# Input rows loaded in longer runs and the contraction index split in pairs, in a gated mix of two attention branches

## The chip, the cores and the metric

The kernel runs on one core of a Trainium2 chip. The core has five engines with a program each: TensorE (PE, with its weight loads listed as PEld), VectorE (DVE), ScalarE (ACT), GpSimd (POOL) and SyncE (SP), which here issues every transfer. The metric is the device time of one execution, in microseconds; lower is better. The time before is the median of three runs, 845.19 us (843.88 to 845.63).

## The reference

The input x has 2048 rows of 512 values in bf16. Two branches read it, and a gate mixes them row by row:

```python
x = A_x
g = _sigmoid((x * gate_w).sum(-1, keepdims=True))
a = _A_ref(x, A_mem0, A_Wq, A_Wk, A_Wv, A_Wo, A_seg_len)
b = _B_ref(x, B_wq, B_wk, B_wv, B_wo, B_beta)
return g * a + (1 - g) * b
```

Branch A goes through 64 segments of 32 rows, one after another. Each puts 8 memory rows ahead of its rows, projects the 40 rows to queries, keys and values of 32 heads of 128, does masked attention, and projects the result back to 512 columns:

```python
for s in range(n_seg):
    h = jnp.concatenate([mem, xs], axis=1)
    q = jnp.einsum('btd,dhe->bhte', h, Wq)      # k and v likewise
    ...
    o = jnp.einsum('bhte,hed->btd', o, Wo)
    mem = o[:, :M, :].copy()
    outs.append(o[:, M:, :])
```

The first 8 rows of a segment's result are the memory of the next. The segments are therefore a chain.

Branch B projects x with three weights of 512 x 512 to 32 heads of 16, does causal attention inside each of 4 blocks of 512 rows, and adds what a running memory of key and value products from the blocks before gives; then it multiplies by wo.

## The kernel before

**Start.** `plan_warm` (L500) lets TensorE multiply zeros, `WARM` = 9 times. `plan_loads` (L515) issues the loads on SP in this order: the first 512 rows of x, the B weights wk, wq and wv, 512 more rows of x, three small inputs (beta, the gate weights, the memory rows), the rest of x. Rows of x lie in `x_sb`, which shares its memory with `Wo_sb`, and the profile calls it by that name; wvB is likewise `woB_sb`. Row tile i holds rows 128 i to 128 i + 127, one to a partition, so a load of two tiles reads runs of one row, 1 KB. The contraction index d of a weight is 128 c + p for partition p and c of 4, so a B weight is read in runs of 1 KB too. The A weights (Wk, Wq, Wv, 4 MB each in four loads of 1 MB with runs of 8 KB) are issued one at a time between the pieces of the B stage.

`x_chunk` (L561) turns 512 rows: for each half of a chunk, 8 transposes on TensorE (L573) write one bank, and two copies bring the bank to `xT`, with d on the partitions. Both copies of half 0 run on ACT (L390) and both of half 1 on DVE (L392). `evac` (L388) is the helper that records all such copies, so they share these two lines.

**B stage.** `b_projections` (L641) makes a list of pieces for the first three blocks. `pk` (L671) projects keys and queries, copies them to a stage tile `stgk` and stores them to DRAM through `store` (L653, the transfer itself is L654). `pv` (L689) projects 128 rows to values, copies them to `V17` and stores these, four stores a block, each in runs of 1,088 bytes. `kn` and `mz` make the running memory `MZ16`, which is stored as well. The main loop of `build` (L404 to L427) calls the pieces in order, and puts the chunks of x, the parts of the gate (`gate_parts`, L598: turn the gate weights, turn the memory rows, four sets of dot products) and the weight loads between them.

**A stage.** `plan_a` (L1251) plays lists of units written out by hand, one list for a group of four segments (`A_LIST0` to `A_LIST15`); every engine's program has the order of these lists. A unit is for instance a projection (L1281), the scores (L1542), P times V (L1607, L1619), the output projection (`out_part`, L1365), or `wl`, which issues one of eight loads of Wo. `LateB` (L767) projects B's last block with weights loaded 128 columns at a time (`load`, L779), and `BAttn` (L845) does B's attention, in the gaps. Scores of queries and keys use every second element of `KT_sb` and `QT_sb`, in which two heads are interleaved.

The output projection leaves four partial sums on four sets of 32 partitions. `fold` (L1376) adds and turns them: its stationary operand is 32 columns of the f32 tile `WF`, its moving operand a stack of identities, 8 matmuls for half the columns (16 in the trace). The copies `hm` put the first 8 rows into the next segment's `hT`, and `atx` and `aTl` put the rest into `aT_st`. That tile goes through DRAM (`aTd`) to `aTg`. `f_atr` in `tail_units` (L1477, the matmuls at L1482) turns it back into rows, 16 matmuls for a group of four segments, and the last step mixes in B's rows and the gate and stores the output.

**Memory.** The tiles of the start (`in_p`) and those of the A stage (`in_a`) lie over each other. `over` (L368) makes the first writer of an A tile wait for the last users of the start's tiles below it. In order of address the start's tiles are wkB, wqB, phK, etmp, bmask, mskT, mem0_sb, gwr_sb, beta_sb, gB_sb, omgB_sb, MZ16, stgk, V17.

SP works through its list in order: an issue that waits holds up all behind it.

Of the kernel before, what the change touches and what calls it, by code (L numbers as in the profile page):

```python
# [10 lines left out]
DEV = dict(nseg_limit=None)  # L11
WARM = 9

# [244 lines left out]
def build(nc, es, A_x, A_mem0, A_Wq, A_Wk, A_Wv, A_Wo, B_wq, B_wk, B_wv, B_wo, B_beta, gate_w, out, dbg=None):  # L258
    v = NS()
# [30 lines left out]
    def alloc(stack, *specs):  # L290
        at, spans = 0, {}
        for name, shape, dt, n in specs:
# [23 lines left out]
    in_p = alloc(esP, ("wkB", [128, C, DM], BF16, 0), ("wqB", [128, C, DM], BF16, 0), ("phK", [128, 4, DM], BF16, 0), ("etmp", [128, 512], BF16, 5),  # L316
          ("bmask", [128, 136], BF16, 0), ("mskT", [128, 2, 8, 2, 2], BF16, 0), ("mem0_sb", [128, DM], BF16, 0), ("gwr_sb", [128, 128], BF16, 0), ("beta_sb", [128, HB], BF16, 0),
          ("gB_sb", [128, HB], F32, 0), ("omgB_sb", [128, HB], F32, 0), ("MZ16", [128, 544], BF16, 0),
# [49 lines left out]
    def over(home):  # L368

        parts = {"mem0_sb": "mem0", "gwr_sb": "gwr", "beta_sb": "beta", "gB_sb": "gB", "omgB_sb": "omgB"}  # L370
        ops = []
        for p in v.under[home]:
            p = parts.get(p, p)
            for n, r in list(R.items()):
                if n == p or p in ("V17", "phK") and n.startswith(p) or p.startswith("stgk") and n[:-1] == p:
                    ops += ([r.w] if r.w else []) + r.readers
        return list({id(o): o for o in ops}.values())
# [27 lines left out]
    for n in range(len(pieces)):  # L405
        if n in (8, 20, 32):
            x_chunk(v, (n + 4) // 12)
        if n == 9:
            sigmoid(v, v.beta_sb[:, :], v.gB_sb, v.omgB_sb, "gB", [Rs("beta")])
            for src, dst, res in ((v.gB_sb, v.gBp, "gB"), (v.omgB_sb, v.omgBp, "omgB")):  # L410
                for j in range(4):
                    q = slice(32 * j, 32 * j + 32)
                    P.op("gp", lambda g, src=src, dst=dst, q=q, j=j: g.tensor_copy(dst[q, :].rearrange("p (f e) -> p f e", e=2), src[q, :].rearrange("p (f j e) -> p f j e", j=4, e=2)[:, :, j, :]),
                         reads=[Rs(res)], writes=[Rs(res + "p")], name="%sp%d" % (res, j))
            v.late_const()
        if n >= 36 and n % 2 == 0 and gates:
            gates.pop(0)()
        pieces[n]()
        if n == len(pieces) - 3:
            v.late_mask()  # L420
        if n in (36, 37, 38, 40, 42):
            bat.load(0, n // 2 % 2 if n != 37 else 0, "kv"[n // 40] if n != 37 else "q")
        if weights and n % 3 == 2:
            weights.pop(0)()
# [90 lines left out]
def plan_loads(v, A_x, A_mem0, A_Wq, A_Wk, A_Wv, B_wq, B_wk, B_wv, B_wo, B_beta, gate_w):  # L515
    P, Rs, C, M = v.P, v.Rs, v.C, v.M
    xsrc = A_x[0].rearrange("(i p) d -> p i d", p=128)

    def ld(grp, dst, src, res, name):
        P.dma(P.group(grp), lambda s: s.dma_start(dst, src), writes=[Rs(res)], name=name)  # L520

    def x(k):
        for h in range(2):
            o = 4 * k + 2 * h
            ld("x%d%d" % (k, h), v.x_sb[:, o:o + 2, :], xsrc[:, o:o + 2, :], "x_sb%d%d" % (k, h), "dma_x%d%d" % (k, h))
    x(0)
    for nm, dst, src in (("wk", v.wkB, B_wk), ("wq", v.wqB, B_wq), ("wv", v.wvB, B_wv)):
        ld("b" + nm, dst[:, :, :], src.rearrange("(c p) n -> p c n", p=128), nm + "B", "dma_" + nm)
    x(1)
    g = P.group("small")  # L530
    for fn, res in ((lambda s: s.dma_start(v.beta_sb[:, :], B_beta.rearrange("(o n) -> o n", o=1).to_broadcast([128, v.HB])), "beta"),
                    (lambda s: s.dma_start(v.gwr_sb[0:C, :], gate_w.rearrange("(c p) -> c p", p=128)), "gwr"),
                    (lambda s: s.dma_start(v.mem0_sb[0:M, :], A_mem0[0]), "mem0")):
        P.dma(g, fn, writes=[Rs(res)], name="dma_" + res)
# [3 lines left out]
    def weight(grp, dst, src, res, c):  # L538
        P.dma(grp, lambda s: s.dma_start(dst[:, c, :], src[c * 128:(c + 1) * 128].rearrange("p h e -> p (h e)")),
              writes=[Rs(res)], name="dma_%s%d" % (res, c))  # L540
# [18 lines left out]


def x_chunk(v, k):  # L561

    P, Rs, BK, C = v.P, v.Rs, v.BK, v.C
    for h in range(2):
# [3 lines left out]
        def f(pe, bk=bk, tiles=tiles):  # L568
            ins = None
            for n, i in enumerate(tiles):  # L570
                for c in range(C):
                    o = (n * C + c) * 128
                    ins = pe.transpose(v.pb16[bk][:, o:o + 128], v.x_sb[:, i, c * 128:(c + 1) * 128], v.ident[:, :])  # L573
            return ins
        P.op("pe", f, reads=[Rs("x_sb%d%d" % (k, h)), Rs("ident")], writes=[v.rbank[bk]], name="xtr%d_%d" % (k, h))
        t0 = 128 * tiles[0]
        dst = v.xT[:, :, t0:t0 + 256].rearrange("p c (n t) -> p n c t", t=128)
        src = v.pb16[bk][:, 0:1024].rearrange("p (n c t) -> p n c t", n=2, c=C)
        for n in range(2):
            v.evac("dve" if h else "act", dst[:, n, :, :], src[:, n, :, :], [bk], [Rs("xT%d_%d%d" % (k, h, n))], "xev%d_%d%d" % (k, h, n))  # L580
        BK.give(bk)
# [16 lines left out]
def gate_parts(v):  # L598

    P, Rs, BK, C, NTT = v.P, v.Rs, v.BK, v.C, v.NTT  # L600
    st = {}

    def weights():
        bk = BK.take()
        P.op("pe", lambda pe, bk=bk: pe.transpose(v.pb16[bk][:, 0:C], v.gwr_sb[0:C, :], v.ident[0:C, 0:C]),
             reads=[Rs("gwr"), Rs("ident")], writes=[v.rbank[bk]], name="gwtr")
        v.evac("dve", v.gw_sb[:, :], v.pb16[bk][:, 0:C], [bk], [Rs("gw")], "gwev")
        BK.give(bk)

# [17 lines left out]
    def memory():  # L627
        bk = BK.take()

        def f_m0tr(pe):  # L630
            ins = None
            for c in range(C):
                ins = pe.transpose(v.pb16[bk][:, c * v.M:(c + 1) * v.M], v.mem0_sb[0:v.M, c * 128:(c + 1) * 128], v.ident[0:v.M, 0:v.M])
            return ins
        P.op("pe", f_m0tr, reads=[Rs("mem0"), Rs("ident")], writes=[v.rbank[bk]], name="mem0tr")
        v.evac("dve", v.hT[0][:, :, 0:v.M], v.pb16[bk][:, 0:C * v.M].rearrange("p (c t) -> p c t", t=v.M), [bk], [Rs("hTm0_0"), Rs("hTm0_1")], "memT0")
        BK.give(bk)
    return [weights, memory] + [lambda k=k: dots(k) for k in range(NTT // 4)]


def b_projections(v):  # L641
# [47 lines left out]
    def pv(sb, tt):  # L689
# [3 lines left out]
        def fp(pe):  # L693
            ins = None
            for c in range(C):
# [4 lines left out]
        v.evac("act", v.V17[:, sb % 2, tt, :, 0:16].rearrange("p (e m) d -> p m e d", e=2), v.pb[bk].rearrange("p (m e d) -> p m e d", e=2, d=16), [bk], [rv], "evv%d_%d" % (sb, tt))  # L700
        store("stv%d" % sb, v.vd[sb, :, tt, :], v.V17[:, sb % 2, tt, :, :].rearrange("p h w -> p (h w)"), [rv, Rs("V17o")], [Rs("vd%d_%d" % (sb, tt))],
              "stv%d_%d" % (sb, tt))
        BK.give(bk)
# [63 lines left out]
class LateB:  # L767
# [11 lines left out]
    def load(self):  # L779
# [6 lines left out]
        m, f = self.work[4 + i]  # L786
        src = (v.B_wk if m == "K" else v.B_wq).rearrange("(c p) n -> p c n", p=128)[:, :, 128 * f:128 * (f + 1)]
        dst = v.woB_sb[:, i % 4, :].rearrange("p (c w) -> p c w", w=128)
        P.dma(P.group("lw%d" % i, "lw%d" % (i % 4)), lambda s: s.dma_start(dst, src), writes=[Rs("woc%d" % (i % 4))] + ([Rs("wvB")] if i < 4 else []), name="ldc%d" % i)

# [460 lines left out]
def plan_a(v, nseg):  # L1251
# [124 lines left out]
    def fold(bk, hf, part, res, name):  # L1376

        def f(pe):
            ins = None
            for n in range(2):  # L1380
                for j in range(4):
                    o = 256 * hf + 128 * n + SEG * j
                    ins = pe.matmul(pb[bk][SEG * j:SEG * (j + 1), SEG * n:SEG * (n + 1)], part[:, o:o + SEG], v.fold[:, :],  # L1383
                                    start=True, stop=True, skip_group_check=True)
# [3 lines left out]
    def folded(bk):  # L1388
        return pb[bk][:, 0:2 * SEG].rearrange("p (c t) -> p c t", t=SEG)

    def ol_units(g):
# [29 lines left out]
        def ut2(bks):  # L1421
            n = 3 if g == ngrp - 1 else 4
            dst = aT_st[par][:, :, :].rearrange("p (a c) (r t) -> p a c r t", a=2, t=SEG)[:, :, :, 0:n, SEG - 8:SEG]
            for hf in range(2):
# [16 lines left out]
    def tail_units(g):  # L1441

        last = g == ngrp - 1
        rows = aT_st[g % 2] if last else aTg
        rr = [Rs("aTl%d" % (g % 2))] + [Rs("aTx%d_%d" % (g % 2, r)) for r in range(4)] if last else [Rs("aTg")]
# [28 lines left out]
        def uf():  # L1474
            bk = B.take()

            def f_atr(pe):  # L1477
                ins = None
                for c in range(C):
                    for j in range(4):  # L1480
                        q = slice(SEG * j, SEG * (j + 1))
                        ins = pe.matmul(pb[bk][q, c * 128:(c + 1) * 128], rows[:, c, q], ident[:, :], start=True, stop=True)  # L1482
                return ins
# [18 lines left out]
    def segment(s):  # L1502
# [152 lines left out]
        def w_rows(hf):  # L1655
            if last:
                dst = aT_st[par][:, :, SEG * r:SEG * (r + 1)].rearrange("p (a c) t -> p a c t", a=2)
                evac(("act", "dve")[hf], dst[:, hf], folded(wb["f%d" % hf]), [wb["f%d" % hf]], [Rs("aTx%d_%d" % (par, r)), Rs("aTl%d" % par)], "atx%d_%d" % (s, hf))
# [4 lines left out]
                return  # L1663
            dst = aT_st[par][:, :, SEG * r:SEG * (r + 1) - M].rearrange("p (a c) t -> p a c t", a=2)
            evac(ENG["ax"], dst[:, hf], folded(wb["f%d" % hf])[:, :, M:SEG], [wb["f%d" % hf]], [Rs("aTx%d_%d" % (par, r))], "atx%d_%d" % (s, hf))
# [164 lines left out]
```

## Time and profile before

| | |
|---|---|
| three runs, median | 845.19 us (843.88 to 845.63) |
| profiled execution, its own time | 845.43 us |
| its span | 843.4 us |
| TensorE busy, share | 811.5 us, 96% |
| chain that ended last, share of TensorE | 85% |
| mean granted clock of TensorE | 0.996 |
| loads of x (8 of 256 KB), issue to landing | 8.2 us median |
| loads of the first Wk, Wq, Wv (4 of 1 MB each) | 10.1, 13.6, 15.4 us median |
| stores of V (12 of 136 KB) | 9.0 us median |
| stores of keys and queries (12 of 256 KB) | 9.7 us median |

The span is one execution recorded by the hardware profiler. Busy time of an engine is the time in which it had an instruction at work. A group of instructions is given with line, engine, operation, tiles, shape and count, then busy time and mean length, then the idle time before it and what ended that. The chain is followed back from the last instruction: at each step to what released it. Matmuls are pipelined, so the length of one in a group (219 ns for 128 columns) is longer than its distance to the next, and the chain shows how long a batch holds the engine.

### The profile page before, as it was taken

Reading aid. Unit: us, or ns where it says so; the run is one execution under the profiler, and the core shown is the slowest. Engines: PE = TensorE matmul, PEld = TensorE weight load, DVE = VectorE, ACT = ScalarE, POOL = GpSimd, SP = SyncE. Lnnn points to the kernel's source line nnn. Section 1 sums busy time; section 2 is a strip of 40 time slices with the busy share of each in tenths; the row PEclk is TensorE's granted clock in tenths of the full one; section 3 lists DMA queues with packets and bytes.
Section 4 is the critical chain, followed back from the end, with each engine's and each line's share of the span. In section 5 each row is a group of like instructions: output and inputs, shape, how many; then the busy total and the mean of one; then the engine's idle time right before and its main releaser. Section 6 shows DMA issues by size and latency. Waiting matters only on the chain.

```text
span 843.4 us, 49436 instructions
## 1 busy us (share of the span) xinstructions
PE 811.5 (96%) x22174; PEld 441.1 (52%) x22174; DVE 572.0 (68%) x1381; ACT 589.8 (70%) x1506; POOL 284.8 (34%) x780
## 2 busy tenths in 40 slices
PE   8997999999999999999999999999999999999997
PEld 4643455555555555555555555555655555555564
DVE  3554457577566767767767777778687787677764
ACT  5545677767777777777677777777767677777544
POOL 3612233333333343333333333333333333434110
PEclk9999899999999999999999999999999999999999
DMA  9996312112002011111012021111112021110111
GB/s 314 419 365 210 73 51 57 54 29 50 28 18 55 24 48 33 46 38 43 19 37 54 20 52 32 47 38 33 36 24 63 18 52 32 36 45 13 33 41 47
DMA packets 84442, 57.50 MB, mean 68 GB/s; under 512 B 55296, under 2 KB 79112, under 8 KB 82696
## 3 DMA queue, kind: packets, MB, share of 16 engines
q1 hardware_dynamic: 84232, 54.36, 21.2%
q8 instruction: 174, 2.85, 1.4%
q14 instruction: 36, 0.29, 0.1%
HBM read 37.14 MB, written 17.20 MB: 64 GB/s over the span
## 4 chain that ended last, share of the span: by engine, by line
PE 85%; ACT 6%; DMA 5%; DVE 2%; issue 1%; SPq 1%; DVEq 0%; POOL 0%; ACTq 0%
PE ps L1281 46%; PE ps L1365 17%; PE ps L1383 3%; PE ps L1607 3%; PE ps L909 2%; PE ps L962 2%; DMA scr_kqd<-stgk 2%; PE ps L1460 2%; PE ps L1542 2%; PE ps L678 1%; PE ps L1577 1%; ACT R_sb L1587 1%; ACT PT L930 1%; DMA Wo_sb<-in_A_Wo_dram 1%; PE ps L813 1%
## 5 line engine op out<-in xcount | busy, mean ns | idle before, releaser
L936 POOL TENSOR_SCALAR_AFFINE_SELECT PT<-PT 128x128 bf16<-128x128 bf16 (+2 forms) x320 | 117.5, 367 | 206.0 <-ACT PT L930 157.7
L930 ACT ACTIVATE PT<-ps 128x512 bf16<-128x512 f32 x320 | 174.9, 610 | 5.4 <-PE ps L909 4.2
L1281 PE MATMUL ps<-Wq_sb,hT 128*32 128x512 bf16 x2048 | 138.1, 383 | 0.4
L1281 PE MATMUL ps<-Wv_sb,hT 128*32 128x512 bf16 x2048 | 138.2, 379 | 0.0
L1281 PE MATMUL ps<-Wk_sb,hT 128*32 128x512 bf16 x2048 | 136.1, 380 | 0.4
L1365 PE MATMUL ps<-Wo_sb,OT_sb 128*32 128x512 bf16 x2048 | 129.9, 381 | 3.9 <-DMA Wo_sb<-in_A_Wo_dram 3.3
L1597 POOL TENSOR_TENSOR P_sb<-P_sb,R_sb 128x64 bf16<-128x64 bf16 x128 | 50.8, 397 | 136.9 <-ACT R_sb L1587 131.1
L390 ACT ACTIVATE OT_sb<-ps 128x320 bf16<-128x320 f32 x170 | 68.7, 435 | 21.8 <-PE ps L1619 20.4
L1281 PEld LDWEIGHTS ps<-Wq_sb,hT 128*32 128x32 bf16 x2048 | 59.1, 97 | 47.0 <-ACT hT L390 2.9
L1281 PEld LDWEIGHTS ps<-Wk_sb,hT 128*32 128x32 bf16 x2048 | 59.4, 97 | 45.8 <-ACT hT L390 2.6
L390 ACT ACTIVATE WF<-ps 128x256 f32<-128x256 f32 x105 | 35.2, 381 | 58.7 <-PE ps L1365 56.4
L1365 PEld LDWEIGHTS ps<-Wo_sb,OT_sb 128*32 128x32 bf16 x2048 | 48.2, 96 | 48.5 <-ACT OT_sb L390 7.5
L1293 DVE STREAM_TRANSPOSE KT_sb<-KN_sb 128x256 f32<-128x256 f32 x128 | 56.5, 441 | 22.2 <-ACT KN_sb L390 19.2
L1293 DVE STREAM_TRANSPOSE QT_sb<-QN_sb 128x256 f32<-128x256 f32 x128 | 56.4, 441 | 22.0 <-ACT QN_sb L390 18.4
L390 ACT ACTIVATE QN_sb<-ps 128x512 bf16<-128x512 f32 x78 | 46.9, 604 | 34.0 <-PE ps L1281 33.3
L390 ACT ACTIVATE KN_sb<-ps 128x512 bf16<-128x512 f32 x75 | 45.0, 602 | 33.2 <-PE ps L1281 32.8
L1556 ACT ACTIVATE P_sb<-ps 128x224 bf16<-128x224 f32 x128 | 45.9, 359 | 28.5 <-PE ps L1547 20.6
L1281 PEld LDWEIGHTS ps<-Wv_sb,hT 128*32 128x32 bf16 x2048 | 50.2, 95 | 23.8 <-issue 0.6
L1591 DVE TENSOR_TENSOR P_sb<-P_sb,R_sb 128x160 bf16<-128x160 bf16 x128 | 42.0, 329 | 20.8 <-ACT R_sb L1587 18.6
L392 DVE CAST V_sb<-ps 128x512 bf16<-128x512 f32 x76 | 51.8, 682 | 5.5 <-PE ps L1281 5.1
L392 DVE CAST OT_sb<-ps 128x320 bf16<-128x320 f32 x86 | 41.1, 487 | 18.7 <-PE ps L1619 17.6
L1607 PEld LDWEIGHTS ps<-P_sb,V_sb 32*128 32x128 bf16 x2048 | 23.4, 91 | 57.6 <-DVE P_sb L1591 26.0
(142 smaller groups left out, 1490.0 us busy)
## 6 DMA issues: line engine op xcount, KB each, us to landing
Wk_sb<-in_A_Wk_dram SPq DMA_DIRECT2D x4, 1024.0 KB, 10.1
Wq_sb<-in_A_Wq_dram SPq DMA_DIRECT2D x4, 1024.0 KB, 13.6
Wv_sb<-in_A_Wv_dram SPq DMA_DIRECT2D x4, 1024.0 KB, 15.4
Wo_sb<-in_A_Wo_dram SPq DMA_DIRECT2D x8, 512.0 KB, 5.7
scr_vld<-VNL SPq DMA_DIRECT2D x16, 256.0 KB, 2.8
VL<-scr_vld SPq DMA_DIRECT2D x64, 64.0 KB
scr_kqd<-stgk SPq DMA_DIRECT2D x12, 256.0 KB, 9.7
Vj<-scr_vd SPq DMA_DIRECT2D x32, 68.0 KB, 2.4
```

The lines of the kernel that those rows point to most:

```text
L390: P.op("act", lambda a: a.activation(dst, src, ACT.Copy), reads=[v.rbank[k] for k in bks], writes=dres, name=name)
L392: P.op("dve", lambda d: d.tensor_copy(dst, src), reads=[v.rbank[k] for k in bks], writes=dres, name=name)
L930: P.op("act", lambda a: a.activation(pt, v.pb[bk], ACT.Exp, scale=v.SCALE_B), reads=[v.rbank[bk]], writes=[rp], name="be%d_%d" % (n, t))
L936: P.op("gp", lambda g: g.affine_select(mv, mv, [[0, len(cut)], [1, 128]], ALU.is_ge, 0.0, base=0, channel_multiplier=-1), reads=[rp], writ ...
L1281: ins = pe.matmul(pb[bk][SEG * j:SEG * (j + 1), :], lhs(c), cols(w, j) if split else w[:, 512 * j:512 * (j + 1)], start=(c == 0), stop=(c ...
L1293: P.op("dve", lambda d: d.transpose(to, src), reads=reads, writes=writes, name=name)
L1365: ins = pe.matmul(pb[bk][SEG * j:SEG * (j + 1), :], lhs(4 * k + j), Wo_sb[:, 4 * k + j, :], start=(first and k == ks[0]), stop=False, skip ...
L1383: ins = pe.matmul(pb[bk][SEG * j:SEG * (j + 1), SEG * n:SEG * (n + 1)], part[:, o:o + SEG], v.fold[:, :], start=True, stop=True, skip_grou ...
L1556: P.op("act", lambda a: a.activation(P_sb[:, b, :], pb[bk][:, 0:224], ACT.Exp, scale=SCALE), reads=[rbank[bk]], writes=[Rs("P%d" % b), Rs( ...
L1591: P.op("dve", lambda d: d.tensor_tensor(wide(P_sb, b)[:, :, 0:L], wide(P_sb, b)[:, :, 0:L], R_sb[:, b, :].rearrange("p (i q) -> p i q", q= ...
L1597: P.op(ENG["n"], lambda d: d.tensor_tensor(left(P_sb), left(P_sb), grp04(R_sb[:, b, :]), ALU.mult), reads=[Rs("R%d" % b)], writes=[Rs("P%d ...
L1607: ins = pe.matmul(pb[bks[j]][:, L * i:L * (i + 1)], V_sb[SEG * j:SEG * (j + 1), b, i * E:(i + 1) * E], P_sb[SEG * j:SEG * (j + 1), b, LW * ...
```

## The change

Rows, weights and columns are assigned to partitions in another order, and with that the runs in DRAM get longer.

- x: in chunk 0, partition p of a half gets rows 2p and 2p + 1 (2 KB runs, two loads as before); in chunks 1 to 3 it gets four neighbouring rows (4 KB runs, one load of 512 KB instead of two). The copies to `xT` put the columns back in the order of the rows, so they write every second or every fourth element.
- The contraction index is d = 256 h + 2 p + n, with c = 2 h + n. The B weights are read in 2 KB runs. The A weights keep their 8 KB runs and four loads, with other rows in each. `by_pairs` gives, for a row of 512 columns, the 128 columns of index c, which are every second element of a half. The transposes of x and of the memory rows, the stationary operand of the fold, and the output of L1482 use it.
- `aT_st` and `aTg` hold the two indices c of a half next to each other (`a_rows`), so the copies into them write, and L1482's stationary operand reads, every second element.
- The gate weights are loaded straight into place, as 256 pairs of values of 2 bytes; the tile gwr_sb, the transpose that turned them and its copy go.
- The value stores of a block become one of 544 KB, issued after the fourth copy, in runs of 4,352 bytes.
- `LateB.load` issues two transfers a weight slice instead of one.
- `WARM` is 7. In chunk 0 each half is copied by ACT and DVE together.
- The lists of the A stage are the same.

```diff
-WARM = 9
+WARM = 7
...
-        if n >= 36 and n % 2 == 0 and gates:
+        if n >= 38 and n % 2 == 0 and gates:
...
+        if k:
+            P.dma(P.group("x%d" % k), lambda s: s.dma_start(v.x_sb[:, 4 * k:4 * k + 4, :], A_x[0, 512 * k:512 * (k + 1)].rearrange("(p i) d -> p i d", i=4)),
+                  writes=[Rs("x_sb%d%d" % (k, h)) for h in range(2)], name="dma_X%d" % k)
+            return
...
-            ld("x%d%d" % (k, h), v.x_sb[:, o:o + 2, :], xsrc[:, o:o + 2, :], "x_sb%d%d" % (k, h), "dma_x%d%d" % (k, h))
+            ld("x%d%d" % (k, h), v.x_sb[:, 2 * h:2 * h + 2, :], A_x[0, 256 * h:256 * (h + 1)].rearrange("(p i) d -> p i d", i=2), "x_sb%d%d" % (k, h), "dma_x%d%d" % (k, h))
...
-        ld("b" + nm, dst[:, :, :], src.rearrange("(c p) n -> p c n", p=128), nm + "B", "dma_" + nm)
+        ld("b" + nm, dst[:, :, :].rearrange("p (h n) m -> p h (n m)", h=2), src.rearrange("(h p n) m -> p h (n m)", h=2, n=2), nm + "B", "dma_" + nm)
...
-                    (lambda s: s.dma_start(v.gwr_sb[0:C, :], gate_w.rearrange("(c p) -> c p", p=128)), "gwr"),
+                    (lambda s: s.dma_start(v.gw_sb[:, :].rearrange("p (h n) -> p h n", h=2), gate_w.rearrange("(h p n) -> p h n", h=2, n=2)), "gw"),
...
-        P.dma(grp, lambda s: s.dma_start(dst[:, c, :], src[c * 128:(c + 1) * 128].rearrange("p h e -> p (h e)")),
+        P.dma(grp, lambda s: s.dma_start(dst[:, c, :], src.rearrange("(a p n) h e -> a n p (h e)", a=2, n=2)[c // 2, c % 2]),
...
+class Pairs:
+    def __init__(self, ap):
+        self.ap = ap.rearrange("p (h t n) -> p h n t", h=2, n=2)
+    def __getitem__(self, key):
+        return self.ap[key[0], key[1] // 2, key[1] % 2, key[2]]
...
-                    ins = pe.transpose(v.pb16[bk][:, o:o + 128], v.x_sb[:, i, c * 128:(c + 1) * 128], v.ident[:, :])
+                    ins = pe.transpose(v.pb16[bk][:, o:o + 128], by_pairs(v.x_sb[:, i, :])[:, c, :], v.ident[:, :])
...
-        dst = v.xT[:, :, t0:t0 + 256].rearrange("p c (n t) -> p n c t", t=128)
+        dst = v.xT[:, :, 512 * k:512 * (k + 1)].rearrange("p c (t n) -> p n c t", n=4)[:, 2 * h:2 * h + 2] if k else v.xT[:, :, 256 * h:256 * (h + 1)].rearrange("p c (t n) -> p n c t", n=2)
...
-            v.evac("dve" if h else "act", dst[:, n, :, :], src[:, n, :, :], [bk], [Rs("xT%d_%d%d" % (k, h, n))], "xev%d_%d%d" % (k, h, n))
+            v.evac("dve" if (n if k == 0 else h) else "act", dst[:, n, :, :], src[:, n, :, :], [bk], [Rs("xT%d_%d%d" % (k, h, n))], "xev%d_%d%d" % (k, h, n))
...
-        store("stv%d" % sb, v.vd[sb, :, tt, :], v.V17[:, sb % 2, tt, :, :].rearrange("p h w -> p (h w)"), [rv, Rs("V17o")], [Rs("vd%d_%d" % (sb, tt))],
-              "stv%d_%d" % (sb, tt))
+        if tt == 3:
+            store("stv%d" % sb, v.vd[sb].rearrange("p t w -> p (t w)"), v.V17[:, sb % 2, :, :, :].rearrange("p t h w -> p (t h w)"),
+                  [Rs("V17_%d_%d" % (sb % 2, t)) for t in range(4)] + [Rs("V17o")], [Rs("vd%d_%d" % (sb, t)) for t in range(4)], "stV%d" % sb)
...
+        for h in range(2):
+            P.dma(grp, lambda s, h=h: s.dma_start(dst[:, h], src[:, h]), writes=[Rs("woc%d" % (i % 4))] + ([Rs("wvB")] if i < 4 else []), name="ldc%d_%d" % (i, h))
...
-                    o = 256 * hf + 128 * n + SEG * j
-                    ins = pe.matmul(pb[bk][SEG * j:SEG * (j + 1), SEG * n:SEG * (n + 1)], part[:, o:o + SEG], v.fold[:, :],
+                    cols = by_pairs(part[:, :])[:, 2 * hf + n, SEG * j:SEG * (j + 1)]
+                    ins = pe.matmul(pb[bk][SEG * j:SEG * (j + 1), SEG * n:SEG * (n + 1)], cols, v.fold[:, :],
...
+    def a_rows(t):
+        return t[:, :, :].rearrange("p c t -> p (c t)").rearrange("p (a t c) -> p a t c", a=2, c=2)
...
-                        ins = pe.matmul(pb[bk][q, c * 128:(c + 1) * 128], rows[:, c, q], ident[:, :], start=True, stop=True)
+                        ins = pe.matmul(by_pairs(pb[bk][q, :])[:, c, :], rows[:, c // 2, q, c % 2], ident[:, :], start=True, stop=True)
```

## The prediction

> **What bounds the kernel now.** I read the engine table and the forty slices of the page first, then the granted clock and the transfer rate by stretches, then the chain that ended last, and last the groups of instructions with shapes kept apart.
>
> ```profile
> PE 811.5 (96%) x22174; PEld 441.1 (52%) x22174; DVE 572.0 (68%) x1381; ACT 589.8 (70%) x1506; POOL 284.8 (34%) x780
> PEclk9999899999999999999999999999999999999999
> DMA  9996312112002011111012021111112021110111
> GB/s 314 419 365 210 73 51 57 54 29 50 28 18 55 24 48 33 46 38 43 19 37 54 20 52 32 47 38 33 36 24 63 18 52 32 36 45 13 33 41 47
> ```
>
> TensorE is busy for 96% of the span, and its clock is full except in the fifth slice (84 to 105 us). The transfer engines are full only in the first three slices. So there are two places: a start of some 85 us in which transfers can hold TensorE up, and 750 us in which the count and the price of TensorE's instructions set the time. The stretches of the start (columns: length, busy time of PE, PEld, DVE, ACT, POOL, clock, transfer share, GB/s):
>
> ```profile
> 2.00:16.00 14.00, 12.88 (x81) 7.04 (x80) 5.56 (x11) 5.33 (x11) 3.70 (x8) 1.00 0.99 324
> 20.00:50.00 30.00, 29.15 (x264) 16.72 (x262) 15.51 (x34) 17.75 (x33) 15.33 (x78) 1.00 1.02 416
> 82.00:89.00 7.00, 6.06 (x84) 2.37 (x88) 0.82 (x2) 2.43 (x6) 0.41 (x1) 0.53 0.33 80
> ```
>
> Both first stretches are full, but the one with 1 KB runs moves 324 GB/s and the one with 8 KB runs 416. The third shows TensorE at 0.53 of its clock. The chain of the first 90 us (start, length, what; its transfers and one copy):
>
> ```profile
> 2.32 6.71 DMA wqB<-in_B_wq_dram
> ...
> 30.61 15.00 DMA scr_kqd<-stgk
> ...
> 49.37 0.64 ACT V L390
> ...
> 56.32 4.09 DMA scr_vd<-V
> ...
> 65.60 5.72 DMA scr_vld<-VNL
> ...
> 75.08 7.29 DMA Wo_sb<-in_A_Wo_dram
> ```
>
> TensorE's own list there:
>
> ```profile
> 82.41 1.04 PE L1365 MATMUL ps<-Wo_sb,OT_sb 128*32 128x512 bf16 x8 [3.26 <-DMA Wo_sb<-in_A_Wo_dram]
> 83.95 0.71 PE L1383 MATMUL ps<-fold,WF 128*32 128x32 f32 x32 [0.49 <-ACT WF L390]
> 84.69 3.60 PE L1281 MATMUL ps<-Wq_sb,hT 128*32 128x512 bf16 x32
> 88.08 2.17 PE L1281 MATMUL ps<-Wk_sb,hT 128*32 128x512 bf16 x32
> ```
>
> What is gained before 82.41 us counts only as far as the last Wo load lands sooner, and behind that wait TensorE runs at half clock. 32 matmuls of 512 columns take 1.73 us at full clock (32 of them, 0.054 us apart), so the half clock costs 1.66 + 0.28 us in the last two lines, 0.43 in the eight of Wo (1.04 for 0.61) and 0.35 in the folds: 2.7 us.
>
> For the 750 us, the groups and two pieces of the late chain:
>
> ```profile
> L1542 PEld LDWEIGHTS ps<-QT_sb,KT_sb 128*32 128x32 bf16 x2048 | 31.9, 95 | 28.2 <-DVE QT_sb L1293 10.5 <-DVE KT_sb L1293 8.2 <-issue 1.2
> L1383 PEld LDWEIGHTS ps<-fold,WF 128*32 128x32 f32 x2048 | 30.9, 111 | 22.4 <-ACT WF L390 9.2 <-DVE WF L392 2.0 <-issue 1.6
> L1482 PE MATMUL ps<-ident,aTg 128*32 128x128 bf16 x240 | 6.3, 219 | 0.3 <-issue 0.3
> ```
> ```profile
> 825.81 0.22 PE ps L1482 x16
> ...
> 826.63 0.12 PE ps L1383 x16
> ```
>
> A group's turning back into rows (L1482) holds the chain for 0.22 us, half a fold (L1383) for 0.12.
>
> **The change, part by part.** The base is the profiled execution, 845.43 us (span 843.4, 2.0 around it), 0.24 above the median of the three runs.
>
> *Longer runs.* By the trace's packet records a run of 1 KB takes one transfer engine 46 ns, 2 KB 84, 8 KB 309; 4 KB by interpolation 159. For each of 16 engines: first 512 KB of x, 32 runs become 16 (1.47 to 1.34 us); the other 1.5 MB, 96 become 24 (4.42 to 3.82); wk, wq, wv, 96 become 48 (4.42 to 4.03); the merged value stores, 96 runs of 1,088 bytes at 48 ns become 24 of 4,352 at 168 (4.61 to 4.04). Together 1.7 us of full transfer engines. The big weights keep 8 KB runs in another row order: nothing. The gate vector becomes 256 runs of 4 bytes; small packets take 9 to 18 ns, so 16 for each engine cost 0.15 to 0.3 us, which nobody waits for before 40 us; I take 0.
>
> *Start of TensorE.* Seven warming matmuls end 0.86 us sooner (two of 0.43); the first rows have landed by 0.81 + 2.8 = 3.6 us, so the transposes begin at 4.2. The two copies of a half run beside each other. DVE's now write every second element: 0.38 us as now, or 0.69 as its copies of 512 from f32 (L392); I take 0.69, and the projections could start at about 6.9 instead of 7.77. But wk lands at 7.3 - 0.26, and the second projection needs wq, which the chain shows at 9.03. wq lands 0.4 us sooner by the sums above, so the start gains 0.4, not 0.86. In the later chunks DVE pays 0.31 us a copy, six times; DVE is busy 15.5 of 30 us there and the projections of a chunk come 5 us after its copies: 0.
>
> *Merged stores.* Nine issues fewer on SP, and the one store waits for the fourth copy of V. Behind it stand weight loads on a queue that is late by its own backlog (15 us to landing at 30.6), so the wait is covered; without that cover it is some 3.5 us for one load. SP's last four value stores take 53.78 to 57.41 us; one takes 0.4 to 1.5, so the Wo loads behind them leave 2 us sooner. The copies of V at 49.37, behind the 15 us store, come sooner too, and TensorE's wait of 0.72 us for them goes. Its lead at the Wo wait is then 0.4 + 0.7 = 1.1 us.
>
> *The Wo wait.* The last loads are issued behind the loads of VL, which wait for the store at 65.60 to land. I let this shift by the transfer time saved: 1.7 us. From below it is 0.4 (only the start's lead, if issue and not bytes sets it), from above 4.4 (the wait of 3.26 gone, and the lead of 1.1). The wait shrinks to 3.26 - 1.7 + 1.1 = 2.7 us, so I take a third of the half clock as gone, 0.9 us of 0 to 2.7. The Trainium skill (TensorE: Matmul & The Clock Gate, Part 1) has the clock halved after an idle window of about 3.4 us whose start is not tied to the kernel. The 0.53 behind 3.26 us of waiting agrees; by that rule the half clock goes in more executions the shorter the wait, and the sum lies between the two ends just given.
>
> *V_sb moved.* Without gwr_sb (256 bytes) the tiles behind it slide, and V_sb lies on MZ16. Its first copy (ACT, 59.64) must then wait for the third MZ store, issued at 57.45 and landed 3.8 us later, at 61.3. With SP 2 us sooner it lands by 59.3: 0; from above 1.7 us of ACT, with the exponentials queued behind it.
>
> *Smaller moves.* A turn of the gate weights goes (0.17 us of TensorE). Eight late weight loads become sixteen: 8 x 0.51 = 4.1 us of SP between 86 and 120, where SP waits 15.6 us for TensorE before just these loads; next behind them are KTj loads, which then wait at most 0.5 us: 0.
>
> *Strided operands of TensorE.* x, mem0 and the attention rows become every second element, as KT_sb and QT_sb are in L1542, where a weight load takes 95 ns against 97 for contiguous ones: 0. With 128 columns no row shows it: from above the three later chunks of 16 transposes at the 1.85 us of the cold first chunk for 1.06, +2.4 us. The fold loads every second f32, which no row shows either: 0 by L1542, from above a second 0.12 us for each of 160 half folds, 19 us. L1482 now writes every second f32 of a bank. Its nearest rows are L1547 and L1619, which write runs of 8 and 16, at 177 and 188 ns for 32 and 64 columns, in line with 181 for 40 contiguous: I take 0, and from above four times its 0.22 us in 16 groups, +10.6. The Trainium skill (PSUM — Partial Sum Buffer, Specifications) says that PSUM's lines are 8 bytes and any non-contiguous pattern slows matmuls significantly. L1547 and L1619 do not show it, but no run there is a single element. That result is a rival below.
>
> *Narrow copies.* The aT_st copies (213 ns on ACT, 197 on DVE) write with a step and come late to nobody: 0.
>
> **Sum:** 845.43 - 1.7 - 0.9 = 842.8; by the median's 0.24, **842.6 us**, 0.3% faster. About 0.2% (1.7 us) is what a measurement here can tell from no change.
>
> **Rivals.**
> *Single f32 elements halve L1482's writing.* If each takes a line of its own, 16 matmuls take 0.44 us for 0.22, in 16 groups +3.5 us on an engine that is the bound: 842.6 + 3.5 = 846.1. It ends slower than before from 0.38 us a group (2.6 / 16 more). For it: L1482's would be the only matmuls that write many lone elements. Against it: broken writes of 8 elements cost nothing. At three times the price the time is 849.6. This is what the Trainium skill's page PSUM — Partial Sum Buffer (Specifications) would have here.
> *The fold pays.* Two passes of weight loads (32 for 16 matmuls) at 111 ns against 95 say that f32 reads are already dearer; if half of the upper price comes, 842.6 + 9.6 = 852. Against it: bf16 with a step is free.
> *The transfers are hidden anyway.* SP's order sets the Wo landing, only 0.4 us comes, the half clock stays; and the start is colder, with TensorE idle from 6.0 to 7.0 and 7.9 to 8.6. Should full clock come at 12 instead of 9 us, half of 3 us is lost: 845.2 - 0.4 + 1.5 = 846.3; with V_sb's wait 848.
>
> **Numbers.** Forecast 0.43 (faster 0.39, same 0.04; its own range, 838.1 to 844.8, from the bounds of the early part, 0.4 to 7.1 us). Single elements 0.27 (0.03, 0.08, slower 0.16, since the price may exceed twice). Fold 0.14 (all slower). Hidden 0.16 (same 0.06, slower 0.10). Together faster 0.42, same 0.18, slower 0.40. The range 839.5 to 850.0 leaves out most of the fold's case and the end where wait and half clock both vanish.
>
> **What would show it.** wqB on the chain landing near 8.6; rates near 350 GB/s or more between 2 and 16 us; the wait at L1365 shorter and its end near 80.5 us; PEclk of the fifth slice; the chain's 0.22 for 16 of L1482 and 0.12 for 16 of L1383 unchanged. The prediction is wrong if either of the last two grows, or if the wait's end stays at 82.

## The result and the profile after

The changed kernel takes 848.27 us (median of nine runs, 846.16 to 850.15). The kernel before took 845.19 us beside it (843.53 to 847.88). The ratio is 1.0034, with a 95% interval of 1.0018 to 1.0050: slower by 2.9 us (1.5 to 4.2), where a gain of 2.6 us was forecast. The profiled execution took 849.0 us, with a span of 846.9 us.

The same four lines of the page, now of the changed kernel:

```profile
PE 814.3 (96%) x22165; PEld 439.6 (52%) x22171; DVE 578.9 (68%) x1380; ACT 594.3 (70%) x1506; POOL 284.1 (34%) x780
PEclk9999899999999999999999999999999999999999
DMA  8996321211102011111012021111112021110111
GB/s 291 420 377 205 79 54 48 62 29 46 32 19 53 24 44 37 46 38 44 19 37 54 19 53 32 46 38 35 34 23 61 20 52 31 37 45 10 35 41 46
```

TensorE is busy 2.8 us longer than before, with nine instructions less. The stretches of the start (same columns as before: length, busy time of PE, PEld, DVE, ACT, POOL, clock, transfer share, GB/s):

```profile
2.00:16.00 14.00, 11.78 (x59) 5.84 (x59) 4.83 (x9) 4.07 (x8) 3.69 (x8) 0.88 0.88 316
20.00:50.00 30.00, 29.55 (x262) 17.05 (x266) 20.02 (x37) 20.96 (x35) 17.29 (x88) 1.00 1.02 419
```

The first stretch moved 316 GB/s and not 350 or more, and TensorE had 0.88 of its clock there for 1.00 before. The chain of the first 90 us in the changed kernel (start, length, what):

```profile
2.19 7.01 DMA wqB<-in_B_wq_dram
9.24 3.57 PE ps L686 x8
...
26.84 2.45 DVE xT L392 x2
...
56.33 5.95 DMA scr_mzd<-MZ
...
67.23 7.45 DMA scr_vld<-VNL
...
78.44 6.96 DMA Wo_sb<-in_A_Wo_dram
```

wqB lands at 9.20 us (9.03 before). The eight projection matmuls behind it take 3.57 us in half clock for 1.90. Two copies to xT and the store of MZ are new steps of the chain. TensorE's list at the Wo wait:

```profile
85.43 1.04 PE L1376 MATMUL ps<-Wo_sb,OT_sb 128*32 128x512 bf16 x8 [2.95 <-DMA Wo_sb<-in_A_Wo_dram]
86.97 0.71 PE L1394 MATMUL ps<-fold,WF 128*32 128x32 f32 x32 [0.49 <-ACT WF L390]
87.71 3.59 PE L1292 MATMUL ps<-Wq_sb,hT 128*32 128x512 bf16 x32
```

The wait ends at 85.43 us, where 80.5 was forecast (82.41 less 1.7 is rather 80.7) and 82.41 was before, and the half clock behind it is still there. The groups that answer to those of before (L1557 was L1542, L1394 was L1383, L1497 was L1482):

```profile
L1557 PEld LDWEIGHTS ps<-QT_sb,KT_sb 128*32 128x32 bf16 x2048 | 32.1, 95 | 28.1 <-DVE QT_sb L1304 10.5 <-DVE KT_sb L1304 8.1 <-issue 0.9
L1394 PEld LDWEIGHTS ps<-fold,WF 128*32 128x32 f32 x2048 | 31.0, 112 | 21.3 <-ACT WF L390 9.1 <-DVE WF L392 1.6 <-ACT aT_st L390 1.3
L1497 PE MATMUL ps<-ident,aTg 128*32 128x128 bf16 x240 | 9.4, 304 | 0.0
```

And the late chain:

```profile
829.38 0.44 PE ps L1497 x16
829.82 0.13 PE ps L1394 x16
```

The fold is unchanged (a weight load of 112 ns for 111, 0.13 us for 16 in the chain against 0.12 to 0.17 before). The row matmuls are not: 304 ns each for 219, and 0.44 us for a group's 16 where the chain had 0.22. That is the price in the first rival, and 16 groups at 0.22 us more are 3.5 us. Two places compete for the loss: these 3.5 us in the tail (the batches of L1497), and the start, where the first of the 128 exponentials of the segments (ACT's L1571, which is L1556 before) begins 1.70 us later than before, and the first behind the Wo wait 2.78 us later.

### The profile page after: what moved, and what is told of

Same layout as the page of the kernel before. It is cut to its first block, busy times and chain, and to the rows that moved or that the text cites. A ratio compares the mean times of both kernels' runs of the same rounds, so it can differ in the third digit from the quotient of the medians.

```text
span 846.9 us, 49417 instructions
## 1 busy us (share of the span) xinstructions
PE 814.3 (96%) x22165; PEld 439.6 (52%) x22171; DVE 578.9 (68%) x1380; ACT 594.3 (70%) x1506; POOL 284.1 (34%) x780
## 4 chain that ended last, share of the span: by engine, by line
PE 87%; ACT 5%; DMA 3%; DVE 2%; issue 1%; SPq 1%; DVEq 0%; ACTq 0%
PE ps L1292 46%; PE ps L1376 17%; PE ps L1394 3%; PE ps L1622 3%; PE ps L920 2%; PE ps L686 2%; PE ps L973 2%; PE ps L1557 2%; PE ps L1475 2%; PE ps L1592 1%; PE ps L704 1%; ACT R_sb L1602 1%; DMA scr_vld<-VNL 1%; ACT PT L941 1%; DMA wqB<-in_B_wq_dram 1%
## 5 line engine op out<-in xcount | busy, mean ns | idle before, releaser
L1571 ACT ACTIVATE P_sb<-ps 128x224 bf16<-128x224 f32 x128 | 45.9, 359 | 28.3 <-PE ps L1562 20.2
```

Of the source, the lines that this page charges most:

```text
L1571: P.op("act", lambda a: a.activation(P_sb[:, b, :], pb[bk][:, 0:224], ACT.Exp, scale=SCALE), reads=[rbank[bk]], writes=[Rs("P%d" % b), Rs( ...
```

## The experiments

Every ratio is against the kernel before, run on the same chip beside the experiment. The changed kernel itself stands at 1.0034.

**Four undoings, one at a time.** First the write in one piece, with the un-pairing left to DVE:

```diff
-  ins = pe.matmul(by_pairs(pb[bk][q, :])[:, c, :], rows[:, c // 2, q, c % 2], ident[:, :], ...)
+  ins = pe.matmul(pb[bk][q, c * 128:(c + 1) * 128], rows[:, c // 2, q, c % 2], ident[:, :], ...)
...
+  for a in range(c.start // 256, c.stop // 256):
+      o = slice(256 * a, 256 * a + 256)
+      w = lambda t: t[:, o].rearrange("p (t n) -> p t n", n=2)
+      ins = dv.scalar_tensor_tensor(w(fin), pb[bk][:, o].rearrange("p (n t) -> p t n", n=2), g_sb[:, g:g + 1], w(t1_sb), ...)
```

> The changed kernel, but the row matmuls of the tail (L1497) write 128 columns in one piece again, and DVE's last step reads the bank with a step of two elements instead (two instructions of 256 elements for one of 512). First theory: the lone f32 elements are what the second half of the span lost. A chain of 16 matmuls goes from 0.40 us back to 0.22, 16 groups give 2.9 us, so about 845.4 us against 848.3, and the drift of +2.2 us against the kernel before that lies after 320 us is gone, while the +1.5 us of before 320 us stays. Rival: the writing is hidden behind DVE's and ScalarE's part of the tail, and the drift has the stepped aT_st copies (ScalarE 213 to 230 ns) as its cause: chain 0.22, but under 0.5 us of time.

Measured: 1.0028 (1.0012 to 1.0044), so no gain that can be told. The matmuls were back at 219 ns, but DVE had more to do. DVE's last step, of this kernel:

```profile
L1511 DVE SCALAR_TENSOR_TENSOR aTg<-ps,g_sb,t_sb 128x256 bf16<-128x256 f32 x32 | 13.9, 475 | 3.7 <-PE ps L1497 2.3 <-ACT t_sb L1483 1.3
```

and of the changed kernel:

```profile
L1506 DVE SCALAR_TENSOR_TENSOR aTg<-ps,g_sb,t_sb 128x512 bf16<-128x512 f32 x15 | 11.1, 743 | 3.0 <-PE ps L1497 2.7
```

Two instructions of 475 ns for one of 743 add 0.21 us a group to DVE, as much as TensorE was given back. Two edits were in this experiment, so it speaks neither for the theory nor against it; it is repeated below without the second. Against that repetition (1.0006, on another chip) the second DVE instruction alone makes 1.0028: that DVE took the gain back is likely, but the two intervals meet, and it is not shown.

x loaded and copied as before:

```diff
-  ld("x%d%d" % (k, h), v.x_sb[:, 2 * h:2 * h + 2, :], A_x[0, 256 * h:256 * (h + 1)].rearrange("(p i) d -> p i d", i=2), ...)
+  ld("x%d%d" % (k, h), v.x_sb[:, o:o + 2, :], A_x[0].rearrange("(i p) d -> p i d", p=128)[:, o:o + 2, :], ...)   # all chunks
...
+  dst = v.xT[:, :, t0:t0 + 256].rearrange("p c (n t) -> p n c t", t=128)
```

> The changed kernel, but x is loaded as before (1 KB runs, two loads a chunk) and the copies to xT write elements side by side again. First theory: the stepped copies are late for TensorE at the start. ScalarE's copies go from 1.20 us back to 0.54 to 0.60 and DVE's from 1.17 to 0.42; the chain's 2.45 us of DVE xT are replaced by under 1 us; the first ScalarE exponential of the sequential part, 1.7 us later than before at 63 us, comes 1.2 to 1.7 us sooner; 1 to 1.5 us of the time, 847. Rival: the copies lie beside the loads and the start is set by wkB and wqB landing: copies as short, exponential and time unmoved (within 0.5 us).

Measured: 1.0063 (1.0046 to 1.0080; six executions), slower and not faster. The copies were short again (0.60 and 0.42 us), yet the first exponential came at 65.0 us, as late as in the changed kernel (64.8). So the stepped copies don't set it. Of the 4.2 us by which this profile is longer than the changed kernel's, 1.0 had come by 320 us; the rest came behind it, where the two kernels have the same instructions. It is taken up again below.

V_sb off MZ16:

```diff
-  ("mem0_sb", [128, DM], BF16, 0), ("beta_sb", [128, HB], BF16, 0),
+  ("mem0_sb", [128, DM], BF16, 0), ("gap_sb", [128, 128], BF16, 0), ("beta_sb", [128, HB], BF16, 0),
```

> The changed kernel with 256 bytes of empty space put where gwr_sb was, so that V_sb no longer lies over MZ16 and doesn't wait for its store. First theory: the chain's step through that store at 56 to 62 us, with TensorE waiting 1.4 us for t_sb, is a cost of its own: the wait goes, the first exponential comes 1.0 to 1.4 us sooner and Wo's landing moves little, 0.5 to 1 us of the time. Rival: the wait for Wo at 82 to 85 us takes up what is saved at 62: the exponential at 63 us is sooner, the one at 91 us is not, time unmoved (within 0.3 us).

Measured: 1.0030 (1.0015 to 1.0045). ScalarE's copy of V_sb in the changed kernel, with its wait:

```profile
62.37 0.60 ACT L390 ACTIVATE V_sb<-ps 128x512 bf16<-128x512 f32 x1 [0.84 <-DMA scr_mzd<-MZ]
```

and with the space:

```profile
60.80 0.63 ACT L390 ACTIVATE V_sb<-ps 128x512 bf16<-128x512 f32 x1
```

The wait was real and is gone, and the first exponential came 0.93 us sooner. The time did not follow: 0.3 us, far inside the interval.

Nine warming matmuls:

```diff
-WARM = 7
+WARM = 9
```

> The changed kernel with nine warming matmuls instead of seven. First theory: the granted clock falls to half at 9.2 us because TensorE stood still for 1.9 us of the 3.4 before, between the warming matmuls and wkB's landing; two warming matmuls more fill 0.8 us of that, the clock stays full in most executions, x's first transposes to projections (3.57 us of half clock in the chain) take 1.9: 0.5 to 1.7 us of the time. Rival: the start waits for the loads of x and the copies anyway: clock full from 6 us on, the exponential at 63 us and the time unmoved (within 0.4 us).

Measured: 1.0035 (1.0022 to 1.0048). TensorE's list with nine:

```profile
9.36 1.04 PE L686 MATMUL ps<-xT,wqB 128*128 128x512 bf16 x4 [0.24 <-DMA wqB<-in_B_wq_dram]
10.23 1.03 PE L686 MATMUL ps<-xT,wkB 128*128 128x512 bf16 x4
```

and with seven:

```profile
9.24 1.89 PE L686 MATMUL ps<-xT,wqB 128*128 128x512 bf16 x4 [0.24 <-DMA wqB<-in_B_wq_dram]
10.93 1.89 PE L686 MATMUL ps<-xT,wkB 128*128 128x512 bf16 x4
```

The half clock at 9 us is gone, as the first theory had it, and in that profile the exponential behind the Wo wait came 3.8 us sooner than in the changed kernel. Again the median did not move. This one execution, though, took 847.64 us, the second shortest of the kernel's twelve (median 849.28).

**The tail by itself.** The changed kernel with the write in one piece and DVE as it was; the un-pairing is left out, so the output's columns stay in the order of the pairs:

```diff
-  ins = pe.matmul(by_pairs(pb[bk][q, :])[:, c, :], rows[:, c // 2, q, c % 2], ident[:, :], ...)
+  ins = pe.matmul(pb[bk][q, c * 128:(c + 1) * 128], rows[:, c // 2, q, c % 2], ident[:, :], ...)
```

> The changed kernel, but the row matmuls of the tail (L1497) write 128 columns in one piece and DVE's last step stays one instruction of 512 elements; the columns of the output are then left in the order of the pairs (the un-pairing of the output is left out, and b's part is added to the wrong columns). In the run with two DVE instructions of 256 elements (476 ns each, against 743 ns for one of 512) the chain of L1497 was back at 0.22 us, but DVE had 0.21 us a group more, and the time didn't move. First theory: that gain of 2.9 us was given back by DVE; with DVE as it was the time is 2.5 to 2.9 us under the changed kernel's, a ratio of 1.000 to the kernel before. Rival: TensorE has slack there, and the drift after 320 us comes from elsewhere: a ratio of 1.003, as with two DVE instructions.

And the kernel before with the stepped write alone, which puts the output's columns into another order:

```diff
-  ins = pe.matmul(pb[bk][q, c * 128:(c + 1) * 128], rows[:, c, q], ident[:, :], ...)
+  ins = pe.matmul(pb[bk][q, :].rearrange("p (h t n) -> p h n t", h=2, n=2)[:, c // 2, c % 2, :], rows[:, c, q], ident[:, :], ...)
```

> The kernel before with one part of the change alone: the row matmuls of the tail (L1482) write lone f32 elements in steps of two (the output's columns then come out in another order; nothing else is left out). First theory: 16 groups at 0.18 us more are 2.9 us, ratio 1.0034, and nearly all of the change's loss. Rival: TensorE has slack there: chain of 0.40 us, but under 0.5 us of time, ratio under 1.0006.

Measured: 1.0006 (0.9990 to 1.0022) for the first, 1.0029 (1.0014 to 1.0044) for the second. Undoing this one line takes the loss away; making it alone brings 2.5 us of it (1.2 to 3.7). (On the same chip the changed kernel with other parts mended, but not this line, is at 1.0042; it comes next.) The chains agree. The changed kernel with the write in one piece:

```profile
827.20 0.22 PE ps L1497 x16
```

and the kernel before with the stepped write:

```profile
826.45 0.44 PE ps L1482 x16
826.89 0.12 PE ps L1383 x16
```

The rival, slack of TensorE in the tail, is out. The 0.40 us of the expectations is 0.44 in the chain.

**The start and the tail mended together.** Space and nine warming matmuls in one kernel:

> The changed kernel with the 256 bytes of empty space before beta_sb and nine warming matmuls together. With the space alone V_sb's wait was gone, but the first eight projection matmuls stood in half clock (3.57 us for 1.90); with nine matmuls alone they took 1.90, but V_sb's wait took up what had been saved. First theory: each hid the other's gain; together the first exponential comes 2 to 2.5 us sooner than in the changed kernel (62.5 us or less), the one behind the wait for Wo 1 to 2 us sooner, time 1 to 2 us less, ratio 1.001 to 1.002. Rival: Wo's landing, which hangs on VNL's store and four issues on SP, takes the rest: exponential at 62.5, the one at 91 us unmoved, ratio 1.003.

Measured: 1.0042 (1.0027 to 1.0057). The first exponential came at 62.7 us, 0.4 sooner than in the kernel before, and the one behind the Wo wait 3.1 us sooner than in the changed kernel. At 103.0 us TensorE then stood before L920. Its waits in this profile (time in all, number, longest):

```profile
PE ps L920 <- DVE P_sb L1575: 1.4, 1, 1.4
```

The changed kernel has no such wait there, and 1.4 of the 3.1 us went at that place. What is gained at the start is partly handed back where TensorE meets an engine that was not early, and none of it was left in the times.

The pairs taken out of the tail on the way through DRAM, on top of the last kernel:

```diff
+  return t[:, :, :].rearrange("p (a c) t -> p a t c", a=2)          # a_rows: side by side
...
+  sp.dma_start(v.aTd[g].rearrange("(a p n) t -> p a n t", a=2, n=2), aT_st[par][:, :, :].rearrange("p (a n) t -> p a n t", a=2))
+  sp.dma_start(aTg[:, :, :], v.aTd[g].rearrange("(c p) t -> p c t", p=128))
...
+  to = by_pairs(pb[bk][q, :])[:, c, :] if last else pb[bk][q, c * 128:(c + 1) * 128]
```

> The changed kernel with the empty space, nine warming matmuls, and the pairs taken out of the tail on the way through DRAM: the rows of aT_st are written side by side, stored to scr_aTd by channel (runs of 512 bytes), and loaded to aTg in the old order of channels (runs of 256 bytes), so that 15 of the 16 groups of L1497 write in one piece and DVE's last step stays one instruction; the last group, which doesn't go through DRAM, keeps its steps. First theory: 15 x 0.18 = 2.7 us and the 1 to 2 us of the start are gained together: 3.7 to 4.7 us under the changed kernel, ratio 0.998 to 0.999, under the kernel before. Rival: the loss sits in neither (random stalls of the two shared engines): ratio 1.002 to 1.003. A third: the load of aTg in 512 runs for 128 comes late and TensorE waits for it: a DMA scr_aTd in the waits of L1497.

Measured: 1.0012 (1.0001 to 1.0024). It is 0.30% under the kernel without the detour, which is 2.5 us for 15 groups; the smaller runs made nobody wait. But it does not beat the kernel before. In its profile the segments at 320 us ran 1.6 us ahead of the kernel before, and at 797 us 1.0 us behind it. Some of that is in a wait for nothing that the profile shows:

```profile
PE ps L1394 <- issue: 1.5, 2, 1.0
```

Over the whole span TensorE's issue waits came to 1.1 us in the profile before, 0.2 in the changed kernel's, 2.5 where x was loaded as before and 1.7 here. Single profiles differ by that much, so a difference of a microsecond between two late stretches is not evidence.

**What is left, each part alone in the kernel before.** x in long runs, with the stepped copies and chunk 0 on both engines:

> The kernel before with one part of the change alone: x in runs of 2 and 4 KB, the stepped copies to xT that these need, and chunk 0's copies on both engines. Undoing just this in the changed kernel gave 1.0063 for 1.0034. First theory: that difference is chance of the executions (waits put down to issue were 2.5 us in the one profile and 0.2 in the other), and the long runs and the stepped copies (1.2 us for 0.4 to 0.6) cancel: the first exponential within 0.7 us of the kernel before, ratio 0.999 to 1.001. Rival: the long runs are worth what undoing them cost: ratio 0.997 to 0.998, and this kernel beats both. A third: the stepped copies cost the 2.45 us that the chain of the changed kernel shows: ratio 1.002.

Seven warming matmuls:

> The kernel before with seven warming matmuls instead of nine, and nothing else. First theory: TensorE stands still longer before wkB lands, the clock is at half when the first eight projection matmuls run (about 3.5 us for 1.90) in most executions, but the transfers that bound the start hide it: the first exponential at most 0.5 us later, ratio 0.999 to 1.001. Rival: the 1.7 us of half clock reach the end: ratio 1.0015 to 1.002.

One value store a block:

> The kernel before with one part alone: the four value stores of a block merged into one of four times the bytes, issued behind the fourth copy. First theory: SP has 12 issues less and the queue is a little sooner free, but the later start of each block's store takes it back: the first exponential within 0.5 us, ratio 0.9995 to 1.0005. Rival, as the prediction had it: 0.7 us of lead that reaches Wo: ratio 0.999. A third: the large store stands ahead of MZ's and makes V_sb late even where it doesn't lie over MZ16: exponential 1 us later, ratio 1.001.

And the changed kernel with all slower parts undone, the tail by the detour:

> The changed kernel with every part undone that a trace showed slower: the pairs taken out of the tail by way of DRAM, 256 bytes of space, nine warming matmuls, and x loaded in 1 KB runs with copies side by side. What is left of the change is B's weights in 2 KB runs, the gate's weights loaded directly, one value store a block and the pairs on the contraction index. First theory: these few are worth nothing to the end: ratio 0.999 to 1.0015, like the same kernel with the long runs of x (1.0012). Rival: the stepped copies were the last loss left, and this one is faster than the kernel before: ratio 0.997 to 0.998.

Their edits are the lines of the change for x, `WARM` and the value store; the last is the kernel with the detour, with x as in the second experiment. Measured: 0.9998 (0.9986 to 1.0011), 1.0005 (0.9991 to 1.0019), 0.9996 (0.9984 to 1.0008) and 1.0010 (0.9995 to 1.0024). Each is no change, and each ratio is that of the first theory. The first exponential was not always: it came 0.68 us later with seven matmuls and 1.22 later with merged stores, where at most 0.5 was expected. No version beats the kernel before.

Two things follow. The 1.0063 of the second experiment does not return when the same undoing is made beside the mended tail (1.0010 with it, 1.0012 without), so it was no price of x's short runs; what it was stays open. And the kernel with merged value stores, whose first 15 us are those of the kernel before, instruction by instruction and with nine warming matmuls, shows this in its profile:

```profile
8.22 1.02 PE L678 MATMUL ps<-xT,wkB 128*128 128x512 bf16 x4 [1.62 <-DMA wkB<-in_B_wk_dram]
9.64 1.89 PE L678 MATMUL ps<-xT,wqB 128*128 128x512 bf16 x4 [0.40 <-DMA wqB<-in_B_wq_dram]
```

So wkB's landing, the wait before it and the half clock behind it differ between executions of one and the same start. Over all fourteen profiles the clock was at half there in five of six with seven warming matmuls and in two of eight with nine. At 13 us this execution was already 2.15 us behind the one before (its first transposes of stgk came at 12.96 for 10.81), and its first exponential came at 64.4 us, nearly as late as the changed kernel's 64.8, while the median of the kernel is that of the kernel before. The 1.70 us at 63 us, which looked like a loss of the change, is thus within what one execution can show.

That does not make a late start free. This execution was the longest of its kernel's twelve (849.11 us, median 846.89). Over the thirteen kernels other than the one before, the profiled execution lies from 2.5 us under its kernel's median to 2.2 over it, and the later its exponential behind the Wo wait, the further over (correlation 0.77). So a late start seems to reach the end of its own execution in large part. What the medians say is that none of the parts moves the start by enough, in all executions, to be told.

## Why the prediction was wrong

The mechanism that decided was named, as the first rival with 0.27, but it was not the forecast. Two steps failed.

*L1482's write, put at 0.* The step took the price from the nearest rows, L1619 and L1547, whose broken runs of 8 and 16 elements (in this order) show no price, and carried it over to runs of one. The runs show 0.44 us for 0.22 in a group of 16, on the engine that is the bound: 3.5 us by the chain, 2.5 (1.2 to 3.7) in the time. The rival said 0.44 and +3.5. By the Trainium skill (PSUM — Partial Sum Buffer, Specifications), where lines are 8 bytes and a non-contiguous pattern slows matmuls significantly, a price was to be expected. The trace now agrees for lone elements with a factor of two, and still disagrees for runs of 8 and 16.

*The 2.6 us of gain at the start and at Wo.* Without them the rival would have given 848.7, and 848.27 was measured. That the two are so close is partly luck, since the tail alone measures 2.5 and not 3.5; and the range of 839.5 to 850.0 holds the result only because it was drawn around the rivals too. Of the parts:

- Longer runs, 1.7 us. The time of the transfer engines was about right; that it shifts the landing of Wo was the step that failed. By the packet records, the loads of x and of B's three weights took 11.1 us of each transfer engine before and 10.1 in the changed kernel (1.1 less was forecast). The merged stores took 4.1 us for about 4.7 (0.6 less was forecast). The price by the run was not quite that of the sum, which used medians: 1 KB runs took 49.6 ns on average, 2 KB 98, so that one step of length gave 1% and not 9%, and 4 KB 159 as put down. But the saving became idle time of the transfer engines. They were busy for 0.88 of the stretch from 2 to 16 us, where it was 0.99, and for 0.67 between 9 and 12 us, where SP's next store, which waits for a projection, was issued at 11.79 for 10.77. The rate did not rise at all, 316 GB/s for 324, and x's part alone is 0.9998.
- The start, 0.4. The projections could not begin at 6.9: wk landed at 7.85 for the 7.0 that was put down, and full clock, which the hidden case had feared at 12 us, came at 12.7. This, too, costs nothing that can be measured (1.0005).
- The lead of 0.7 from merged stores: 0.9996 alone.
- V_sb, put at 0 with 1.7 from above. The store of MZ was issued 1.1 us sooner and not 2 (56.33 for 57.45), and stood behind the merged value store; it took 5.95 us to land for 3.75, and the wait came: V_sb was copied at 62.37 for 59.64. Undoing it moved the ratio from 1.0034 to 1.0030, which is nothing that can be told.
- Wo's landing, 1.7, and half clock, 0.9. The wait ended 3.0 us later, not 1.7 sooner: VNL's store was issued 1.6 us later in that execution (67.23 for 65.60) and landed 1.7 us more slowly (7.45 for 5.72), and the last loads of Wo stand behind it. Why it landed more slowly is not shown. Where the wait ended nearly as early as before (82.87 with the space and nine matmuls), the median was still that of the changed kernel.

What held: transposes from every second element take 0.89 us for 16 as before; the fold is unchanged, so the rival in which it pays is out; and the narrow copies cost 17 ns more (230 for 213), with which the changed kernel without the stepped write is still at 1.0006.

One more size was wrong without harm. DVE's copies to xT were put at 0.69 and ScalarE's at nothing new. They took 0.73 with a step of two, and 1.30 to 1.42 us on both engines with a step of four. The two groups in the changed kernel, and before:

```profile
L390 ACT ACTIVATE xT<-ps 128x512 bf16<-128x512 bf16 x8 | 8.8, 1204 | 4.9 <-PE ps L589 4.9
L392 DVE COPY xT<-ps 128x512 bf16<-128x512 bf16 x8 | 8.8, 1174 | 5.9 <-ACT xT L390 4.9 <-PE ps L589 0.9
```
```profile
L390 ACT ACTIVATE xT<-ps 128x512 bf16<-128x512 bf16 x8 | 4.3, 596 | 5.7 <-PE ps L573 5.7
L392 DVE COPY xT<-ps 128x512 bf16<-128x512 bf16 x8 | 3.0, 420 | 6.8 <-PE ps L573 6.7
```

The projections do not come 5 us behind them everywhere: the chain of the changed kernel holds 2.45 us of them at 26.84. But with the long runs alone the time is 0.9998.

## What to carry to other kernels

A row that shows a broken access pattern to be free holds for its own run length: before a change splits an output into single elements on the engine that is the bound, price it at twice, and count the groups. Time of the transfer engines saved in a transfer-bound start is worth nothing until timed runs show it at the end: it can turn into idle time of these engines, other engines and the landing of the next load can take it back, and one execution's start can differ by more than the saving. When one part is undone by moving its work to another engine, a time that does not move proves nothing; leave the work out instead.

## What was not expected of the hardware

- A matmul of 32 rows by 128 columns that writes every second f32 of a PSUM bank holds TensorE twice as long as one that writes in one piece (0.44 us for 0.22 in 16), while a stationary operand with the same step costs nothing in bf16 or f32 (95 ns, 112 ns a load).
- Copies of 512 bf16 elements whose output has a step of 4 bytes take 0.73 us, and with 8 bytes 1.30 to 1.42, against 0.42 on VectorE and 0.60 on ScalarE side by side. The Trainium skill (SBUF — State Buffer, Door 1: The DMA port swizzle, the note on cachelines) would have steps of up to 8 bf16 elements free. ScalarE's copies disagree at both steps and VectorE's at least between the two; TensorE's reads with a step of two agree.
- The clock's fall to half at 7.5 to 9.5 us came with seven warming matmuls and with nine, behind waits of 1.6 to 2.9 us, but it stayed away behind one of 2.5 us (nine matmuls) and behind one of 1.75 us for the copies (seven). All seven falls came behind waits shorter than the idle window that the prediction goes by, and the length of the wait alone doesn't decide it. The granted clock changed in steps of 3.41 us: at the start and at Wo, half clock lasted 3.41 or 6.83 us in every profile. What sorts all fourteen starts is how long TensorE was busy in the first such step at full clock: 0.94 to 1.58 us in the seven in which the clock then fell, 1.62 to 2.29 in the seven in which it stayed. Near the Wo wait the same count does not sort the profiles (it fell behind 1.97 us and stayed behind 1.89), so this is an observation on these starts and no rule.
